# Two early row tiles turned by DMA instead of TensorE, and the order of the work around the first block's second query projection

## The chip, the cores and the metric

The kernel runs on one core of one Trainium2 chip. The metric is the device time of one execution in microseconds (us); less is better. Engines: PE is TensorE (PEld its weight loads), DVE is VectorE, ACT is ScalarE, POOL is GpSimd, SP is SyncE, which here only issues DMA. DMA transfers run on 16 DMA engines; those issued by SP show as queue q1, those issued by POOL as queue q0.

## The reference

The input x is 2048 rows of 640. It is normalized over its columns, and two branches read the result: attention with 32 heads of width 192 against given keys and values of 2048 rows, and a gated feed-forward layer of width 1536. Cut to what matters:

```python
xn = _layernorm(x, axis=-1)
q = (xn @ wq)                      # 32 heads of 192
scores = q @ k_cache^T * 192**-0.5
p = softmax(scores, axis=-1)
s = (p @ v_cache) @ wo             # A
g = silu((silu(xn @ w1) * (xn @ w3)) @ w2)   # B
return x + s * g
```

All inputs are bfloat16.

## The kernel before, in words

The rows of x come as 16 tiles of 128. Each tile is normalized in its natural layout and then turned, so that xnT holds its 640 columns on the partitions (five blocks of 128 columns), since the projections contract over them. The 2048 query rows are worked in four blocks (qb) of 512, that is four row tiles each. The heads run one after another; within a head and a block, the keys go in eight pairs of 128-row tiles. For each pair, `scores` issues six matmuls into a two-bank PSUM tile, `weights` takes the exponential on ScalarE, and `values` returns two closures ("parts") of eight matmuls each which add to two output banks. The two-bank tile comes from a pool of two buffers (`st2`) that the scores, the projections and the turns share in rotation; the third scores of the start borrow an output bank.

TensorE and most other instructions are pinned (`pin`): each engine runs them in the order in which the program emits them. This order was written by hand. The change lies in the first 50 us, in head 0, where the normalization of the later tiles runs beside the attention of the first block.

Normalizing a tile has these steps, each a small function:

- `load_x(eng, t0, t1)` loads tiles t0 to t1-1 (L188).
- `ln_stats(i)` issues two `ln_half`, each a statistics instruction over half the columns (L213), the second with an aggregate (L215), on VectorE.
- `ln_root(i0, n)` takes the reciprocal root of n tiles' variances on ScalarE, as a logarithm (L243) and an exponential (L250).
- `ln_scale(i0, n)` subtracts the mean and scales, on VectorE, into an `xn` buffer (L261; a pool of four).
- Then the tile is turned, in one of two ways. `next_turn(i0, cp)` makes ten transposes on TensorE for two tiles into PSUM (L270), and copies each tile to xnT with the engine given (L271). `ln_send(i0, n)` scales and issues one DMA transpose per tile from SP's queue, from `xn` straight to xnT (L282).

`first_project(h, qb, *mid)` projects the queries of head h for block qb through `project_chunk`. For head 0 and qb > 0 it uses `by_halves` (L328): ten matmuls, then a small copy as a fence (`mark`, L334; on ScalarE for block 1, on VectorE for the others) that waits for them, then whatever `between` emits, and then ten matmuls that wait for the fence. The results are cast on ScalarE into qA and qF (L361, L362), POOL makes the shifted copies qS and qD, VectorE takes maxima, and `next_bound` makes the block's shift for the exponential. For other heads the 20 matmuls run at L359 and read also xnS, a copy of xnT with its halves swapped, which `swap_rows` makes by DMA from POOL's queue (L380).

`lead()` is the hand-written start of block 0: pairs 0 to 4, with the statistics of tiles 4 to 11 and the turning of tiles 4 to 7 between. Behind it, `advance` takes the further pairs; it keeps up to three parts waiting (four with an extra step) and emits the rest. `extra_at` hangs an extra step on a pair, `posts` hangs steps behind it. Before, the projection of block 1 hung on pair (0, 5), with the root of tiles 8 to 10 and the sending of 8 and 9 in its middle.

Ahead of `lead()` stand, on SP's queue, the loads of x for tiles 8 to 11 and 12 to 15, and on POOL's queue the weights of head 1 and the swap of block 0 (`loads[1] = load_weights(1)`, `swap_rows(0)`).

Of the kernel before, what the change touches and what calls it, by code (L numbers as in the profile page):

```python
# [30 lines left out]
def _kernel_impl(ctx, tc, A_x, A_k_cache, A_v_cache, A_wq, A_wo, B_w1, B_w3, B_w2, out):  # L31
    nc = tc.nc
    _, SQ, D = A_x.shape
    _, H, SK, dh = A_k_cache.shape
# [7 lines left out]
    NPAIR = NKT // 2  # L42
# [111 lines left out]
    with ExitStack() as actx:  # L154
# [32 lines left out]
        def load_x(eng, t0, t1):  # L187
            pin(eng.dma_start(out=x_all[:, t0:t1, :], in_=x2[t0 * P:t1 * P, :].rearrange("(t p) d -> p t d", p=P)))  # L188
# [7 lines left out]
        loads[0] = load_keys(0, [first_w["pieces"][0], lambda: [f() for f in first_w["pieces"][1:]], lambda: [load_x(nc.sync, t, t + 2) for t in (4, 6)]])  # L196
        loads[0].update(first_w)
        load_x(nc.sync, 8, 12)
        load_x(nc.sync, 12, 16)

        fill = ps_o.tile([P, 2, 512], F32, tag="ob1", name="fill")

# [14 lines left out]
        def ln_stats(i):  # L217
            for a in range(nsub):
                ln_half(i, a)
# [36 lines left out]
        def ln_scale(i0, n=2):  # L256
            scaled[i0] = []
            for i in range(i0, i0 + n):
                xn = xnp.tile([P, D], BF16, tag="xn", name="xn")
                act = i in ASUM  # L260
                pin(nc.vector.tensor_scalar(out=xn[:], in0=x_all[:, i, :], scalar1=a_col(nmean, i) if act else mv[:, i, 0:1],  # L261
                                            scalar2=rstd[i], op0=ALU.add if act else ALU.subtract, op1=ALU.mult))
                scaled[i0].append(xn)
# [11 lines left out]
        def next_turn(i0, cp):  # L275
            for copy in ln_turn(i0, (cp, cp)):
                copy()
# [41 lines left out]
        def by_halves(banks, w, qs, touch, between):  # L319
            def behind_of(op, dep):  # L320
                tc.add_manual_dep(op.ins, dep.ins.name, mybir.DependencyInfo(
                    mybir.DependencyClass.Sync, mybir.DependencyReason.DATA), reason="bank")

            for half in range(2):
                for c in range(DC):
                    for r in range(2):
                        t = r ^ half
                        mm = pin(nc.tensor.matmul(banks[t], lhsT=w(t, c)[ROWS[r], :], rhs=xnT[ROWS[r], c, qs],  # L328
                                                  start=(half == 0 and c == 0), stop=(half == 1 and c == DC - 1)))
                        if half == 1 and c == 0:  # L330
                            behind_of(mm, fence)
                if half == 0:
                    mark = fsb.tile([P, 1], F32, tag="mark", name="mark")
                    fence = pin(touch(out=mark[:], in_=eps_t[:]))  # L334
                    behind_of(fence, mm)
                    between()

        def project_chunk(h, qb, cast=nc.vector.tensor_copy, mid=()):
            hd = heads[h]
            wq = hd["L"]["wq"]  # L340
            qA, qF, qS, qD, st = hd["qA"], hd["qF"], hd["qS"], hd["qD"], hd["st"]
            qs = slice(qb * 512, (qb + 1) * 512)
            ps = ps_st.tile([P, 1024], F32, tag="st2", name="ps")
            halves = [ps[:, 0:512], ps[:, 512:1024]]
            if h == 0 and qb > 0:
                by_halves(halves, lambda t, c: wq[:, t, c, :], qs, nc.scalar.copy if qb == 1 else nc.vector.tensor_copy, steps((parts.pop(0),), *mid))
            elif h == 0:
                acc["bp"] = ps_o.tile([P, 2, 512], F32, tag="ob0", name="bp")
                halves[1] = acc["bp"][:, 1, :]
                for u in (slice(0, 256), slice(256, 512)):  # L350
                    for t in range(2):
                        for c in range(DC):
                            pin(nc.tensor.matmul(halves[t][:, u], lhsT=wq[:, t, c, :], rhs=xnT[:, c, u],
                                                 start=(c == 0), stop=(c == DC - 1)))
            else:
                for s in range(2 * DC):
                    for t in range(2):
                        xs = xnT if s % 2 == t else xnS
                        pin(nc.tensor.matmul(halves[t], lhsT=wq[ROWS[t], s, :], rhs=xs[ROWS[t], s // 2, qs],  # L359
                                             start=(s == 0), stop=(s == 2 * DC - 1)))  # L360
            pin(cast(out=qA[:, qs], in_=halves[0]))  # L361
            pin(cast(out=qF[:, qs], in_=halves[1]))  # L362
            keep = pin if h == 0 or h == 1 else (lambda x: x)
            for t in range(2):
                keep(nc.gpsimd.tensor_copy(out=qS[ROWS[t], qs], in_=qA[ROWS[1 - t], qs]))  # L365

            first = h == 0 and qb == 0
            copy = nc.scalar.copy if first else nc.gpsimd.tensor_copy
            keep(copy(out=qD[:, qs], in_=qF[PGW:P, qs]))

            def maxima():
                for col, src, r0 in ((3, halves[0] if first else qA[:, qs], 0), (4, halves[1] if first else qF[:, qs], PGW)):
                    pin(nc.vector.tensor_reduce(out=st[r0:P, col, qb:qb + 1], in_=src[r0:P, :], axis=AX.X, op=ALU.max,
                                                apply_absolute_value=True))
            return maxima
# [110 lines left out]
        def weights(st2, nb):  # L486
            pT2 = pp.tile([P, 1024], BF16, tag="pT2", name="pT2")
            pin(nc.scalar.activation(out=pT2[:], in_=st2[:], func=ACT.Exp, scale=SCALE, bias=nb[:]))  # L488
            return pT2
# [107 lines left out]
        def steps(*fs):  # L597
            return lambda: [f(*a) for f, *a in fs]

        def lead():  # L600
            hd, nb = heads[0], heads[0]["nb"][0]
            vals = [values(hd, 0, p, weights(st2, nb), p < 2) for p, st2 in enumerate(early)]
            for i in (4, 5, 6, 7):
                ln_stats(i)
            ln_half(8, 0)
            vals[0].pop(0)()
            vals.append(values(hd, 0, 3, weights(scores(hd, 0, 3), nb)))
            vals[1].pop(0)()
            ln_root(4, 4)
            st2 = scores(hd, 0, 4)  # L610
            vals.append(values(hd, 0, 4, weights(st2, nb)))
            for v in vals[:4]:
                while v:
                    v.pop(0)()
            for i in (4, 6):
                ln_scale(i)
            ln_half(8, 1)
            next_turn(4, nc.scalar.copy)
            next_turn(6, nc.vector.tensor_copy)
            for v in vals[4]:  # L620
                v()
            for i in (9, 10):
                ln_stats(i)
            ln_half(11, 0)

        posts = {
            (0, 5): ((ln_send, 10, 1), (ln_half, 11, 1)),
            (1, 0): ((ln_root, 11, 1), (ln_send, 11, 1)),
            (1, 2): ((ln_stats, 12), (ln_stats, 13), (swap_rows, 1)),
            (1, 3): ((ln_stats, 14), (ln_stats, 15), (swap_rows, 2)),  # L630
            (2, 1): ((swap_rows, 3),),
        }
        extra_at = {
            (0, 5): ((first_project, 0, 1, (ln_root, 8, 3), (ln_send, 8)),),
            (1, 1): ((first_project, 1, 0),),
            (1, 4): ((first_project, 0, 2, (ln_root, 12, 4), (ln_send, 12), (ln_send, 14)),),
            (2, 1): ((first_project, 1, 1),),
            (2, 4): ((first_project, 0, 3),),
            (3, 1): ((first_project, 1, 2),),
            (3, 4): ((first_project, 1, 3),),  # L640
        }
# [3 lines left out]
        for qb in range(NQB):  # L645
            if qb == 0:
                lead()
            for p in range(5 if qb == 0 else 0, NPAIR):
                ex = extra_at.get((qb, p))
                advance(heads[0], qb, p, steps(*ex) if ex else None)  # L650
                if (qb, p) in behind_at:
                    behind.pop(0)()
                for f, *a in posts.get((qb, p), ()):
                    f(*a)
                if (qb, p) == (1, 5):
                    heads[1]["L"].update(load_keys(1, hold=True))
                if (qb, p) in ((1, 5), (1, 6), (1, 7)):
                    heads[1]["L"]["rest"].pop(0)()
                if (qb, p) == (2, 6):
                    loads[2] = load_keys(2, hold=True)  # L660
                    pin(nc.vector.memset(loads[2]["KT"][:, :, 0:2], 0.0))
                    loads[2]["rest"].pop(0)()
                if (qb, p) == (2, 7):
                    copy_keys(heads[1]["L"])
                    loads[2].update(load_weights(2))
                if (qb, p) in key_at:
                    next_keys(1, key_slots)
                if (qb, p) == (3, 6):
                    finish_head(1)
# [445 lines left out]
```

## Time and profile before

| | us |
|---|---|
| median of 3 runs | 1938.49 (1938.24 to 1938.61) |
| profiled execution, its own time | 1938.35 |
| its span, first to last instruction | 1936.6 |
| TensorE busy | 1927.2 |
| ScalarE busy | 1214.5 |
| VectorE busy | 1094.5 |
| GpSimd busy | 459.9 |

A profile line of the timeline has start, duration, engine, line, operation, what it writes and reads, and the count of instructions merged in it; in brackets stands how long the engine had been idle before it and what ended that. Lines with a q behind the engine's name (SPq, POOLq) are DMA issues. The granted TensorE clock is 0.999 of full over the run.

### The profile page before, as it was taken

To read this page: it belongs to the slowest core of one execution; us is meant where nothing else is said; L and a number is where in the kernel's file an instruction comes from. 1 tells how busy PE (TensorE), PEld (TensorE's weight loads), DVE (VectorE), ACT (ScalarE), POOL (GpSimd) and SP (SyncE) were. 2 spreads that over 40 slices of the span, in tenths; PEclk is the share of its full clock that TensorE was granted. 3 is DMA by queue.
4 is the path that set the end of the run, shared out by engine and by line. 5 is a ranking of instruction groups with operands and counts; after the bars stand their busy time and mean duration, and the time that the engine had idled before them with its cause. 6 is when DMAs were issued, how large, how long until landed. Compare 5 with 4: busy or idle time off the path is not lost.

```text
span 1936.6 us, 59523 instructions
## 1 busy us (share of the span) xinstructions
PE 1927.2 (100%) x26720; PEld 1264.5 (65%) x26743; DVE 1094.5 (57%) x2240; ACT 1214.5 (63%) x1173; POOL 459.9 (24%) x757
## 2 busy tenths in 40 slices
PE   9999999999999999999999999999999999999998
PEld 5666666666666666666666677666666666454455
DVE  8665666565656565656665666656665655521111
ACT  7777777777767677777777777777777777210000
POOL 3432222222222222233222222222222210000000
PEclk9999999999999999999999999999999999999999
DMA  8721223121212222232222222212131102937763
GB/s 171 134 71 41 80 42 79 42 71 39 63 37 68 49 57 60 58 95 68 63 50 71 50 71 49 71 41 79 42 79 41 39 10 94 270 81 146 164 152 76
DMA packets 340375, 148.34 MB, mean 77 GB/s; under 512 B 291649, under 2 KB 333601, under 8 KB 340113
## 3 DMA queue, kind: packets, MB, share of 16 engines
q1 hardware_dynamic: 327152, 114.84, 25.8%
q0 software_dynamic: 8256, 24.58, 4.7%
q10 hardware_dynamic: 4704, 5.05, 0.8%
q8 instruction: 211, 3.46, 0.8%
q14 instruction: 52, 0.42, 0.1%
HBM read 54.26 MB, written 31.98 MB: 45 GB/s over the span
## 4 chain that ended last, share of the span: by engine, by line
PE 99%; SPq 0%; DMA 0%; POOL 0%; ACT 0%; issue 0%; DVE 0%
PE obank L528 35%; PE st L482 34%; PE ps L359 14%; PE ps_s L885 8%; PE ps_s L841 3%; PE ps_f L905 2%; PE ps_gu L698 1%; PE ps_f L921 1%; PE ps L723 0%; PE ps L328 0%; DMA KT<-in_A_k_cache_dram 0%; SPq L114 0%; PE ps_gu L328 0%; SPq L98 0%; PE pst L270 0%
## 5 line engine op out<-in xcount | busy, mean ns | idle before, releaser
L488 ACT ACTIVATE pT<-st,nb 128x1024 bf16<-128x1024 f32 x1016 | 1131.8, 1114 | 434.2 <-PE st L482 433.7
L528 PEld LDWEIGHTS <-pT 64*128 64x128 bf16 x16384 | 713.1, 94 | 242.6 <-ACT pT L488 1.5
L528 PE MATMUL obank<-vt,pT 64*128 64x193 bf16 x16384 | 851.8, 243 | 0.1
L498 DVE COPY osum<-obank 128x386 f32<-128x386 f32 x256 | 142.4, 556 | 548.7 <-PE obank L528 548.5
L482 PE MATMUL st<-qS,KM 64*128 64x512 bf16 x1023 | 384.6, 376 | 0.7 <-ACT qF L362 0.5
L482 PE MATMUL st<-qS,KT 64*128 64x512 bf16 x1023 | 384.6, 376 | 0.1
L482 PE MATMUL st<-qA,KM 64*128 64x512 bf16 x1023 | 384.7, 376 | 0.0
L482 PE MATMUL st<-qD,KT 64*128 64x512 bf16 x1023 | 384.7, 376 | 0.0
L482 PE MATMUL st<-qF,KT 64*128 64x512 bf16 x1023 | 384.6, 376 | 0.0
L482 PE MATMUL st<-qA,KT 64*128 64x512 bf16 x1023 | 384.6, 376 | 0.0
L365 POOL COPY qS<-qA 64x512 bf16<-64x512 bf16 x256 | 189.4, 740 | 513.7 <-DVE qA L361 481.9
L482 PEld LDWEIGHTS <-KT 64*128 64x128 bf16 x4096 | 201.4, 94 | 136.2 <-issue 0.6
L359 PE MATMUL ps<-xnT,wq 64*128 64x512 bf16 x1240 | 288.0, 376 | 0.0
L359 PE MATMUL ps<-xnS,wq 64*128 64x512 bf16 x1240 | 287.0, 376 | 0.0
L359 PEld LDWEIGHTS <-wq 64*128 64x128 bf16 x2480 | 120.1, 94 | 116.6
L505 DVE TENSOR_TENSOR ostage<-osum,rl_all 128x384 bf16<-128x384 f32 x256 | 152.6, 596 | 8.8
L885 PE MATMUL ps_s<-oT,wo_sb 128*128 128x512 bf16 x705 | 154.9, 379 | 0.8
L499 DVE TENSOR_TENSOR osum<-osum,obank 128x386 f32<-128x386 f32 x256 | 142.6, 557 | 8.9
L885 PEld LDWEIGHTS <-wo_sb 128*128 128x128 bf16 x720 | 70.5, 98 | 84.9 <-issue 0.2
L384 DVE TENSOR_REDUCE st<-KT 128x1 f32<-128x512 bf16 (+1 forms) x189 | 122.0, 685 | 1.2
L482 PEld LDWEIGHTS <-KM 64*128 64x128 bf16 x2048 | 100.6, 94 | 17.2 <-issue 1.1
L103 POOL DMA_DIRECT2D wq<-in_A_wq_dram x62 | 45.8, 739 | 272.6 <-PE ps L359 260.3
(136 smaller groups left out, 1179.9 us busy)
## 6 DMA issues: line engine op xcount, KB each, us to landing
o_scr<-ostage SPq DMA_DIRECT2D x64, 384.0 KB, 2.9
vt<-in_A_v_cache_dram SPq DMA_DIRECT2D x62, 384.0 KB, 4.9
wo_sb<-in_A_wo_dram POOLq DMA_DIRECT2D x1, 7680.0 KB, 31.7
wq<-in_A_wq_dram POOLq DMA_DIRECT2D x31, 160.0 KB, 3.3
hT_scr<-hblk SPq DMA_DIRECT2D x16, 256.0 KB, 3.0
xnS<-xnT POOLq DMA_DIRECT2D x8, 320.0 KB, 7.0
wq<-in_B_w_dram POOLq DMA_DIRECT2D x31, 80.0 KB, 2.6
wq<-in_A_wq_dram POOLq DMA_DIRECT2D x31, 80.0 KB, 2.9
```

The lines of the kernel that those rows point to most:

```text
L103: keep(nc.gpsimd.dma_start(out=wq[ROWS[t], :, c0:c1], in_=w.rearrange("(s p) d -> p s d", p=DT)))
L359: pin(nc.tensor.matmul(halves[t], lhsT=wq[ROWS[t], s, :], rhs=xs[ROWS[t], s // 2, qs], start=(s == 0), stop=(s == 2 * DC - 1)))
L365: keep(nc.gpsimd.tensor_copy(out=qS[ROWS[t], qs], in_=qA[ROWS[1 - t], qs]))
L384: pin(nc.vector.tensor_reduce(out=heads[h]["st"][:, j, k:k + 1], in_=heads[h]["L"]["KT"][:, j, c0:c1], axis=AX.X, op=ALU.max, apply_absolu ...
L482: pin(nc.tensor.matmul(st2[:, t * 512:(t + 1) * 512], lhsT=k, rhs=q[ROWS[t], qs], start=(s == 0), stop=(s == 2)))
L488: pin(nc.scalar.activation(out=pT2[:], in_=st2[:], func=ACT.Exp, scale=SCALE, bias=nb[:]))
L498: pin(nc.vector.tensor_copy(out=osum[:], in_=ov[:, 0, :, 0:DH + 1]))
L499: pin(nc.vector.tensor_tensor(out=osum[:], in0=osum[:], in1=ov[:, 1, :, 0:DH + 1], op=ALU.add))
L505: pin(nc.vector.tensor_tensor(out=ostage[:, b * 2:b * 2 + 2, hg * DH:(hg + 1) * DH], in0=osum[:, :, 0:DH], in1=rl.unsqueeze(2).to_broadcas ...
L528: pin(nc.tensor.matmul(acc["o"][b][:, r, (j % 2) * 256:(j % 2) * 256 + DH + 1], lhsT=pT2[ROWS[r], t * 512 + j * P:t * 512 + (j + 1) * P], ...
L841: pin(nc.tensor.matmul(ps, lhsT=oT[:, k, :], rhs=wo_sb[:, k, c0:c1], start=(k == 0), stop=(k == OC - 1)))
L885: pin(nc.tensor.matmul(ps_of[d], lhsT=wo_sb[:, k, d * P:(d + 1) * P], rhs=part(k // KQ)[:, k % KQ, :], start=(k == 0), stop=(k == OC - 1)))
```

## The change

Tiles 4 and 5 get a root of their own, between the exponentials of pairs 1 and 2, and go by `ln_send` (DMA transpose) instead of `next_turn`. Tiles 6 and 7 get a root behind the scores of pair 4 and are still turned on TensorE, in one PSUM tile, copied by VectorE. The load of tiles 12 to 15 is issued behind the two DMA transposes instead of behind the load of 8 to 11. Pair 5's scores and exponential go ahead of the projection of block 1, pair 6's between its halves; the root of 8 to 10 and the sending of 8 and 9 go behind the projection, and the parts of pairs 4 to 6 behind that. `posts` of (0, 5) hang on (0, 7). In `project_chunk`, `by_halves` no longer pops a part by itself; for blocks 2 and 3 the caller passes it (`next_part`).

```diff
@@ start of the program @@
         load_x(nc.sync, 8, 12)
-        load_x(nc.sync, 12, 16)
@@ project_chunk @@
-                by_halves(halves, ..., steps((parts.pop(0),), *mid))
+                by_halves(halves, ..., steps(*mid))
@@ lead @@
+        def next_part():
+            parts.pop(0)()
+
         def lead():
             hd, nb = heads[0], heads[0]["nb"][0]
-            vals = [values(hd, 0, p, weights(st2, nb), p < 2) for p, st2 in enumerate(early)]
-            for i in (4, 5, 6, 7):
-                ln_stats(i)
+
+            def pair(p, st2=None):
+                if st2 is None:
+                    st2 = scores(hd, 0, p)
+                return values(hd, 0, p, weights(st2, nb), p < 2)
+
+            vals = [pair(p, st2) for p, st2 in enumerate(early[:2])]
+            ln_stats(4)
+            ln_stats(5)
+            ln_root(4, 2)
+            vals.append(pair(2, early[2]))
+            ln_half(6, 0)
+            ln_send(4)
+            ln_half(6, 1)
+            ln_stats(7)
+            load_x(nc.sync, 12, 16)
+            vals[0].pop(0)()
+            vals.append(pair(3))
+            vals[1].pop(0)()
+            st2 = scores(hd, 0, 4)
             ln_half(8, 0)
-            vals[0].pop(0)()
-            vals.append(values(hd, 0, 3, weights(scores(hd, 0, 3), nb)))
-            vals[1].pop(0)()
-            ln_root(4, 4)
-            st2 = scores(hd, 0, 4)
-            vals.append(values(hd, 0, 4, weights(st2, nb)))
+            ln_root(6, 2)
+            vals.append(pair(4, st2))
             for v in vals[:4]:
                 while v:
                     v.pop(0)()
-            for i in (4, 6):
-                ln_scale(i)
+            ln_scale(6)
             ln_half(8, 1)
-            next_turn(4, nc.scalar.copy)
             next_turn(6, nc.vector.tensor_copy)
-            for v in vals[4]:
-                v()
+            vals.append(pair(5))
             for i in (9, 10):
                 ln_stats(i)
             ln_half(11, 0)
+            first_project(0, 1, (lambda: vals.append(pair(6)),))
+            ln_root(8, 3)
+            ln_send(8)
+            for v in vals[4:]:
+                parts.extend(v)
+            for _ in range(4):
+                next_part()
 
         posts = {
-            (0, 5): ((ln_send, 10, 1), (ln_half, 11, 1)),
+            (0, 7): ((ln_send, 10, 1), (ln_half, 11, 1)),
...
         extra_at = {
-            (0, 5): ((first_project, 0, 1, (ln_root, 8, 3), (ln_send, 8)),),
...
-            (1, 4): ((first_project, 0, 2, (ln_root, 12, 4), (ln_send, 12), (ln_send, 14)),),
+            (1, 4): ((first_project, 0, 2, (next_part,), (ln_root, 12, 4), (ln_send, 12), (ln_send, 14)),),
...
-            (2, 4): ((first_project, 0, 3),),
+            (2, 4): ((first_project, 0, 3, (next_part,)),),
...
-            for p in range(5 if qb == 0 else 0, NPAIR):
+            for p in range(7 if qb == 0 else 0, NPAIR):
```

More of the change, by code (lines that the diff above doesn't have):

```diff
@@ L345, in project_chunk @@
             if h == 0 and qb > 0:
-                by_halves(halves, lambda t, c: wq[:, t, c, :], qs, nc.scalar.copy if qb == 1 else nc.vector.tensor_copy, steps((parts.pop(0),), *mid))
+                by_halves(halves, lambda t, c: wq[:, t, c, :], qs, nc.scalar.copy if qb == 1 else nc.vector.tensor_copy, steps(*mid))
             elif h == 0:
```

## The prediction

> **What bounds the kernel now.** I read the page first, then the list of who waited for whom on TensorE, then the timelines of TensorE, ScalarE, VectorE and the SP queue from 11 to 48 us, and last the packets of each DMA queue in stretches of that time.
>
> ```profile
> PE 1927.2 (100%) x26720; PEld 1264.5 (65%) x26743; DVE 1094.5 (57%) x2240; ACT 1214.5 (63%) x1173; POOL 459.9 (24%) x757
> PE 99%; SPq 0%; DMA 0%; POOL 0%; ACT 0%; issue 0%; DVE 0%
> ```
>
> ```profile
> PE fill L205 <- DVE cols L170: 1.6, 1, 1.6
> PE st L482 <- ACT qF L362: 0.5, 1, 0.5
> ```
>
> TensorE is busy for 1927.2 of 1936.6 us and is 99% of the chain that ended last. Its list of waits has, behind the start, one entry of 0.5 us at 26 us and two smaller ones. So nothing later gives lost time back: what the first 40 us lose or gain on TensorE stands in the total one for one. A change here is worth the TensorE work that it removes, less the waits that it makes.
>
> **What the change removes from TensorE.**
>
> ```profile
> 17.43 2.18 PE L528 MATMUL obank<-vt,pT 64*128 64x193 bf16 x48
> 19.54 1.33 PE L270 MATMUL pst<-ident_bf,xn 128*128 128x128 bf16 x20
> 22.29 1.26 PE L328 MATMUL ps<-xnT,wq 64*128 64x512 bf16 x10
> 24.02 1.24 PE L328 MATMUL ps<-xnT,wq 64*128 64x512 bf16 x10
> 37.69 0.61 PE L328 MATMUL ps<-xnT,wq 64*128 64x512 bf16 x4
> ```
>
> The 20 transposes of tiles 4 to 7 occupy 19.54 to 20.80, 1.26 us; ten of them go, 0.63 us. With the 0.5 us wait for qF gone too, and some 0.3 us around the fence, the gain could not pass 1.5 us. That is the bound on the good side, and it is less than 0.2% of the time (3.88 us, about what a measurement of this kernel can tell from no change).
>
> Order matters more than work. Before, two parts of pair 4 and the scores of pair 5 stood between the turns and the projection of chunk 1 (22.29). After, the parts go behind the projection, pair 5's scores alone stay ahead, and pair 6 stands between its halves. TensorE runs its list in order, so whatever the first half waits for stops everything. It needs tiles 6 and 7 from VectorE's copies and tiles 4 and 5 from the DMA.
>
> **The near inputs: ScalarE and VectorE.**
>
> ```profile
> 14.26 2.12 ACT L488 ACTIVATE pT<-st,nbb 128x1024 bf16<-128x1024 f32 x2 [1.39 <-DVE nbb L427]
> ...
> 18.27 0.30 ACT L243 ACTIVATE lv<-mv,eps_t 128x4 f32<-128x4 f32 x1
> ...
> 18.71 1.10 ACT L488 ACTIVATE pT<-st,nbb 128x1024 bf16<-128x1024 f32 x1
> ...
> 25.30 0.59 ACT L361 CAST qA<-ps 128x512 bf16<-128x512 f32 x1 [0.91 <-PE ps L328]
> ```
>
> ```profile
> 15.17 0.83 DVE L213 BATCH_NORM_STATS2 st<-x_all 128x6 f32<-128x320 bf16 x2
> 16.04 0.21 DVE L215 BATCH_NORM_AGGREGATE mv<-st 128x2 f32<-128x12 f32 x1
> ...
> 18.84 1.51 DVE L261 TENSOR_SCALAR xn<-x_all,mv,rstd 128x640 bf16<-128x640 bf16 x4 [0.25 <-ACT rstd L250]
> 20.27 0.48 DVE L213 BATCH_NORM_STATS2 st<-x_all 128x6 f32<-128x320 bf16 x1
> ...
> 20.92 0.87 DVE L271 COPY xnT<-pst 128x640 bf16<-128x640 bf16 x2
> ...
> 24.43 0.80 DVE L261 TENSOR_SCALAR xn<-x_all,mv,rstd 128x640 bf16<-128x640 bf16 x2 [0.25 <-ACT rstd L250]
> ...
> 28.96 0.21 DVE L215 BATCH_NORM_AGGREGATE mv<-st 128x2 f32<-128x12 f32 x1
> 29.31 0.56 DVE L498 COPY osum<-obank 128x386 f32<-128x386 f32 x1
> ...
> 37.47 0.15 DVE L334 COPY mark<-eps_t 128x1 f32<-128x1 f32 x1
> ```
>
> A root costs ScalarE 0.44 us (18.27 to 18.71). The early root of 4 and 5 can start at about 16.3, when tile 5's statistics end (16.04 + 0.21) and the two exponentials end (14.26 + 2.12). It pushes the exponential of pair 2 back by 0.44, so the third bank frees later and the 48 matmuls of 17.43 start at about 17.85. VectorE fills the gap with half of tile 6 and scales tile 4 from about 16.88 to 17.27 (1.51 / 4 each), tile 5 to 17.65. The rest of 6, tile 7 and half of 8 follow, about 1 us per tile; the root of 6 and 7 then starts near 19.4, their scaling ends near 20.75, the other half of tile 8 near 21.35, and the two copies (0.87) near 22.25. On TensorE the ten transposes end at about 21.05 and pair 5's scores at 21.7. So without any DMA wait the projection starts at about 22.3, where it starts now: the saved 0.63 us lies in a wait for VectorE.
>
> ScalarE loses two copies there, no longer on anyone's path. A VectorE copy of a turned tile is 0.43 against its 0.65, which is priced already.
>
> **The far input: two transposes by DMA.** Tile 4's can be issued at about 17.35 (the scaled tile plus the 0.07 us that 24.43 + 0.40 to 24.90 shows). What they cost depends on what is in the DMA engines then.
>
> ```profile
> 11.51 1.56 SPq L188 DMA_DIRECT2D x_all<-in_A_x_dram  x2
> 24.90 1.57 SPq L282 DMA_TRANSPOSE xnT<-xn  x1
> 38.56 2.87 SPq L282 DMA_TRANSPOSE xnT<-xn  x1
> 41.53 1.91 SPq L282 DMA_TRANSPOSE xnT<-xn  x1
> ```
>
> ```profile
> xnT<-xn SPq DMA_TRANSPOSE x1, 2.7
> xnT<-xn SPq DMA_TRANSPOSE x1, 7.8
> xnT<-xn SPq DMA_TRANSPOSE x1, 5.4
> ```
>
> The three landing times belong to the issues at 24.90, 38.56 and 41.53. The first met idle engines. The other two followed the swaps that POOL issued, and landed at 46.36 and 46.93. The queues show why; the stretches are 12 to 18, 18 to 24.5 and 36 to 42 us (packets, MB, share of the 16 engines):
>
> ```profile
> q1 hardware_dynamic: 2395, 2.05, 105.2%
> q0 software_dynamic: 14, 0.06, 2.3%
> ```
>
> ```profile
> q0 software_dynamic: 338, 0.93, 70.2%
> ```
>
> ```profile
> q0 software_dynamic: 355, 1.24, 87.7%
> q1 hardware_dynamic: 53, 0.01, 1.6%
> ```
>
> ```profile
> 13.20 1.04 POOL L103 DMA_DIRECT2D wq<-in_A_wq_dram  x1
> 15.67 1.38 POOL L380 DMA_DIRECT2D xnS<-xnT  x2
> ...
> 35.21 2.88 POOL L380 DMA_DIRECT2D xnS<-xnT  x4
> ```
>
> POOL issues head 1's weights from 13.20 and two swaps from 15.67 to 17.05, but its queue moves 0.06 MB before 18: the loads that SP issued earlier go first. From 36 to 42 it is the other way round: a transpose issued at 38.56 moves 0.01 MB until the swaps are through. Here the engines serve in order of issue.
>
> Moving the load of 12 to 15 (0.66 MB of the 2.05 that took 6 us) lets POOL's 0.93 MB start about 1.9 us sooner: about 16 to 21, its stragglers to 22.3. Tile 4's transpose at 17.35 comes 0.3 us behind the last of it, as that of 38.56 came 0.5 us behind the last of the swaps issued to 38.09, and as much lies ahead of it. So I take the contended pair, the nearest rows: tile 5 lands 41.53 + 5.4 - 38.56 = 8.37 us after tile 4's issue, at 25.72, and the projection starts at 25.75. The other bound is two transposes alone, 1.67 us apart (the second of the pair at 24.90 was issued at 26.57): 17.35 + 1.67 + 2.7 = 21.7, no wait. TensorE then stands from 21.7 to 25.75, with nothing to cover it. First term: 25.75 - 22.29 = **3.46 us**.
>
> SP has the load of 12 to 15 queued behind the transposes. Even issued at 23 it lands long before its statistics, which now start at 33.39 and start later after: nothing.
>
> **Behind the projection.** The casts came 3.01 us after its first matmul (25.30 - 22.29); after, pair 6's scores take the place of the part, its exponential ends as the second half ends: 3.0 again. From there VectorE is the chain: maxima, bound, tile 10 and 11, two evictions, statistics of 12 to 15 and the fence of chunk 2 at 37.47, with one gap of 0.14 (28.96 + 0.21 to 29.31); chunk 2's second half starts right behind that fence (37.69). The change puts the scaling of 8 and 9 (0.80) from ahead of the maxima to behind them, inside this run. Less the gap: **0.6 us**. Tile 11's transpose lands about 13 us after the projection starts and chunk 2 wants it after about 14: nothing, by a small margin. POOL's copies and its bound stand as far behind the casts as before. The parts taken at chunks 2 and 3 are only called otherwise: nothing.
>
> Sum: 3.46 + 0.6 = 4.06 us. The profiled execution took 1938.35 us (span 1936.6 and 1.75 around it), 0.14 below the median of the runs; 1938.35 + 4.06 = **1942.4 us**.
>
> **Rivals.** *The queues share.* If the engines alternate between the queues, each transpose loses about 1 us to POOL's packets: tile 5 lands near 21.7 + 1.5 = 23.2, and the loss is 0.9 + 0.6 = 1.5: 1939.9 us, not slower. It decides at a landing before 25.5. The rows of 12 to 18 and 36 to 42 speak against it; for it, stragglers of both queues run together after 18. By the Trainium skill (DMA: Bandwidth & Descriptors, Queues, rings and completion order) each engine does go round the queues packet by packet; by that rule the time would be near this rival's, and the two stretches do not agree with it.
>
> *The clock falls.*
>
> ```profile
> 1.65 1.86 PE L205 MATMUL fill<-ones_w,ones_bf 128*128 128x512 bf16 x4 [1.65 <-DVE cols L170]
> 6.67 0.81 PE L205 MATMUL fill<-ones_w,ones_bf 128*128 128x512 bf16 x3
> ```
>
> After the idle start the fills run about 0.43 us apart, later about 0.22. If TensorE comes out of a 4 us wait at that half rate for as long as at the start (some 3.4 us: 4.72 us for 13 fills), the projection loses 1.7 us more: 4.06 + 1.7 = 5.8, 1944.1 us. Against it: no wait of this length stands in the trace. The Trainium skill (TensorE: Matmul & The Clock Gate, Part 1) has the clock halve after an idle window of about 3.4 us that runs free; the cold fills agree with its rate, and no row here shows a fall inside the kernel.
>
> *The DMA is early.* Both land by 22.3, and only VectorE's 0.6 or a part of the 1.5 us gain is left: -0.5 to +0.6, 1938.4 us. It needs POOL's queue empty at about 20.
>
> *Tile 11 late.* Should the swaps of chunk 1 overtake its transpose, chunk 2 waits 1 to 2 us more: about 1944.
>
> **How the numbers follow.** Forecast 0.42, of which 0.28 above the bound and 0.14 below, since 4.06 stands so near 3.88; clock 0.17; sharing 0.24; early 0.10; tile 11 late 0.05; and 0.02 for a gain of over 0.2% that no row explains. Slower 0.28 + 0.17 + 0.05 = 0.50; same 0.14 + 0.24 + 0.10 = 0.48; faster 0.02. The range goes from 1938.7 (early, with VectorE's part) to 1945.3 (clock, 1.2 us more for a later landing). The likeliest case alone: 1941.3 to 1943.4.
>
> **What would show it.** Right: a TensorE wait of about 4 us ahead of the first L328 near 22, ended by the DMA of xnT; POOL's queue from 16, tile 4's packets only after 20; the first half at 25 to 26, chunk 2's second half at 41 to 42. Sharing: both transposes landed by 24. Clock: L328 matmuls at double spacing behind the wait. Wrong altogether: a projection that starts by 22.3.

## The result, and the profile after

The changed kernel takes 1942.97 us (median of 14 runs, 1940.58 to 1944.84), the kernel before 1938.54 us (14 runs, 1938.12 to 1939.48). The ratio is 1.0022, 95% interval 1.0014 to 1.0029: slower by 4.43 us. The profiled execution took 1943.48 us, its span is 1941.7 us (1936.6 before). Not only the median moved: the runs spread over 4.3 us where those of before spread over 1.4.

The page's busy times and its chain, and TensorE's list of waits (who waited for whom: total us, times, longest):

```profile
PE 1928.7 (99%) x26710; PEld 1266.3 (65%) x26733; DVE 1093.9 (56%) x2240; ACT 1212.9 (62%) x1173; POOL 458.5 (24%) x757
PE 98%; DVE 1%; DMA 0%; ACT 0%; issue 0%; POOL 0%
```

```profile
PE ps L327 <- DMA xnT<-xn: 2.8, 1, 2.8
PE fill L204 <- DVE cols L170: 1.6, 1, 1.6
PE ps L327 <- DVE mark L333: 0.5, 1, 0.5
```

Ten matmuls fewer were issued, yet TensorE was busy 1.5 us longer. Two waits are new: 2.8 us for the DMA ahead of block 1's projection, and 0.5 us for VectorE's fence at block 2's. TensorE's timeline:

```profile
25.13 1.82 PE L327 MATMUL ps<-xnT,wq 64*128 64x512 bf16 x10 [2.82 <-DMA xnT<-xn]
...
27.99 1.81 PE L327 MATMUL ps<-xnT,wq 64*128 64x512 bf16 x10
29.62 1.51 PE L527 MATMUL obank<-vt,pT 64*128 64x193 bf16 x32
...
42.95 1.25 PE L327 MATMUL ps<-xnT,wq 64*128 64x512 bf16 x10 [0.52 <-DVE mark L333]
```

The ten matmuls that took 1.24 to 1.26 us before take 1.8 now. The stretches of 1 us show why; behind the busy times and counts of PE, PEld, DVE, ACT and POOL stand the granted TensorE clock, the DMA engines' share and GB/s:

```profile
25.00:26.00 1.00, 0.87 (x8) 0.51 (x10) 0.00 (x0) 0.00 (x0) 0.00 (x0) 0.84 1.07 361
26.00:27.00 1.00, 1.00 (x8) 0.42 (x6) 0.00 (x0) 0.01 (x1) 0.00 (x0) 0.50 0.25 81
28.00:29.00 1.00, 1.00 (x8) 0.52 (x6) 0.00 (x0) 0.73 (x1) 0.00 (x0) 0.50 0.00 0
29.00:30.00 1.00, 1.00 (x18) 0.63 (x15) 0.00 (x0) 0.54 (x2) 0.00 (x0) 0.95 0.07 16
```

The clock is half from about 25.68 (0.84 of that stretch) to 29.1 (0.95), that is for 3.4 us. It fell half a microsecond after the wait had ended. The projection, with pair 6's scores between its halves, took 4.49 us (25.13 to 29.62, where the next matmuls start).

The wait itself, on SP's queue, with the times from issue to landing of the two transposes behind it, and the queues in the stretches 18 to 19, 20 to 21 and 21 to 22 us:

```profile
17.68 2.75 SPq L281 DMA_TRANSPOSE xnT<-xn  x1
20.52 1.22 SPq L281 DMA_TRANSPOSE xnT<-xn  x1
```

```profile
xnT<-xn SPq DMA_TRANSPOSE x1, 6.7
xnT<-xn SPq DMA_TRANSPOSE x1, 4.5
```

```profile
q0 software_dynamic: 62, 0.13, 96.4%
q1 hardware_dynamic: 8, 0.01, 6.7%
...
q0 software_dynamic: 61, 0.20, 99.5%
q1 hardware_dynamic: 8, 0.00, 1.5%
...
q1 hardware_dynamic: 192, 0.05, 81.7%
q0 software_dynamic: 49, 0.15, 63.1%
```

Tile 4's transpose is issued at 17.68 and moves next to nothing until about 21, while POOL's weights and swap keep the engines busy for 96 to 100%; what is left of them (49 packets in the stretch to 22) then moves beside it. Tile 5's transpose lands at 25.0.

The sum can be closed on the timelines. Before, block 2's second half started at 37.69, now at 42.95: 5.26 us. The first scores came 0.35 later (12.98 against 12.63), ahead of anything that the change touches. The projection starts 12.15 us after them instead of 9.66: 2.49. The half clock gives 1.7 (below), VectorE's longer run the remaining 0.7. From there on nothing is lost or won: from the second half of block 3's projection to the end are 1883.92 us before (1936.6 - 52.68) and 1883.76 after (1941.7 - 57.94).

### The profile page after: what moved, and what is told of

Same layout as the page of the kernel before. It is cut to its first block, busy times and chain, and to the rows that moved or that the text cites. A ratio compares the mean times of both kernels' runs of the same rounds, so it can differ in the third digit from the quotient of the medians.

```text
span 1941.7 us, 59510 instructions
## 1 busy us (share of the span) xinstructions
PE 1928.7 (99%) x26710; PEld 1266.3 (65%) x26733; DVE 1093.9 (56%) x2240; ACT 1212.9 (62%) x1173; POOL 458.5 (24%) x757
## 3 DMA queue, kind: packets, MB, share of 16 engines
q8 instruction: 211, 3.46, 0.8%
## 4 chain that ended last, share of the span: by engine, by line
PE 98%; DVE 1%; DMA 0%; ACT 0%; issue 0%; POOL 0%
PE obank L527 35%; PE st L481 34%; PE ps L358 14%; PE ps_s L903 8%; PE ps_s L859 3%; PE ps_f L923 2%; PE ps_gu L716 1%; PE ps_f L939 1%; PE ps L741 0%; DVE st L212 0%; PE ps L327 0%; DMA xnT<-xn 0%; DVE xn L260 0%; DMA x_all<-in_A_x_dram 0%; PE ps_gu L327 0%
```

## Experiments

The theory: the two transposes come behind what POOL put into the DMA engines, TensorE idles, its clock falls, and VectorE's scaling of tiles 8 and 9 lengthens its run to block 2's fence. The rivals: DMA transposes are slow beside any traffic, the queues share by packets, or the new order itself costs the time. The differences below are between medians, each against the kernel before on the same chip. Where the interval of the ratio holds 1, the median alone doesn't tell the run from the kernel before, and the reading rests on the timelines, one profiled execution for each run.

**The swap behind tile 5.**

```diff
         loads[1] = load_weights(1)
-        swap_rows(0)
...
             load_x(nc.sync, 12, 16)   # in lead(); ahead of it:
+            behind5 = stt.tile([P, 1], BF16, tag="behind5", name="behind5")
+            pin(nc.gpsimd.tensor_copy(out=behind5[:], in_=xnT[:, DC - 1, 6 * P - 1:6 * P]))
+            swap_rows(0)
```

> The change, with POOL's swap of block 0 issued only once tile 5 has landed (a one-column copy on POOL reads it first). Theory (the two transposes wait for what POOL put into the DMA engines before them): without the swap only 0.33 MB of weights lies ahead, tile 5 lands near 22, the wait of 2.8 us ahead of the projection shrinks to under 0.5 us, TensorE's clock stays up, and the total is 1938.8 to 1939.5 with a narrow spread. Rival (a DMA transpose is slow by itself beside any traffic, or the queues share by packets): the wait stays above 2 us and the total above 1941.

Measured: 1939.49 us against 1938.76 (+0.73; ratio 1.0004, 0.9995 to 1.0013), 1938.65 to 1940.51. The transposes, and TensorE's waits:

```profile
17.84 1.25 SPq L281 DMA_TRANSPOSE xnT<-xn  x1
19.18 2.11 SPq L281 DMA_TRANSPOSE xnT<-xn  x1
```

```profile
xnT<-xn SPq DMA_TRANSPOSE x1, 4.2
xnT<-xn SPq DMA_TRANSPOSE x1, 3.5
```

```profile
PE ps L327 <- DVE mark L333: 0.5, 1, 0.5
PE pst L269 <- DVE xn L260: 0.3, 1, 0.3
PE ps L327 <- DVE xnT L270: 0.3, 1, 0.3
```

Tile 5 lands at 22.68, the 2.8 us wait is gone, and the projection starts 9.62 us after the first scores, as before (9.66). Of the 4.43 us, 3.7 hang on POOL's swap, which the change did not touch. What is left is VectorE's longer run, with the wait for the fence at its end.

**All four tiles on TensorE, in the new order.**

```diff
-            ln_send(4)
+            ln_scale(4)
...
+            next_turn(4, nc.scalar.copy)
             next_turn(6, nc.vector.tensor_copy)
```

> The change's order, but tiles 4 and 5 are turned on TensorE in a bank of their own ahead of 6 and 7, copied by ScalarE, instead of by DMA. Theory (the DMA is the cost, the order is not): no wait for a DMA, the projection of block 1 starts near 22.6 to 23 us, the total is 1938.9 to 1939.8. Rival (the new order itself, with the parts behind the projection, costs most): 1941 or more.

Measured: 1940.34 us (+1.58; 1.0008, 0.9999 to 1.0017), 1939.82 to 1940.62. Higher than expected, but far from the rival's 1941. The projection starts 10.12 us after the first scores; block 2's fence is late by 0.2, and pair 5's scores wait for a bank that ScalarE must first copy:

```profile
PE st L481 <- ACT xnT L270: 0.5, 1, 0.5
```

So the new order costs 1.58 us when TensorE also turns tiles 4 and 5, more than the 0.73 with two DMA transposes that have only head 1's weights ahead of them. Turning by DMA was not in itself the loss; what lay ahead of it in the DMA engines was.

**Matmuls in the wait.**

```diff
+            if h == 0 and qb == 1:      # in project_chunk, ahead of by_halves
+                for _ in range(12):
+                    pin(nc.tensor.matmul(halves[0], lhsT=ones_bf[:], rhs=ones_w[:], start=True, stop=True))
```

> The change, with twelve matmuls that compute nothing needed put on TensorE between pair 5's scores and the projection (2.6 us at full clock), so that TensorE isn't idle in the wait. Theory (the wait makes the clock fall to half for some 3.4 us, worth 1.7 us in most runs): the wait shows only a rest under 1 us, the clock stays at 1.0 from 25 to 30 us, the total falls to about 1941.2 and the spread of 4 us between runs shrinks to under 2. Rival (the slow matmuls behind the wait have another cause, such as the DMA traffic): the matmul spacing stays and the total stays near 1943.

Measured: 1941.96 us (+3.20; 1.0016, 1.0007 to 1.0026), with all runs between 1941.52 and 1942.94. TensorE's timeline, and the stretches 24 to 26 and 26 to 28 us:

```profile
25.59 1.25 PE L327 MATMUL ps<-xnT,wq 64*128 64x512 bf16 x10 [0.38 <-DMA xnT<-xn]
27.33 1.24 PE L327 MATMUL ps<-xnT,wq 64*128 64x512 bf16 x10
28.41 1.50 PE L530 MATMUL obank<-vt,pT 64*128 64x193 bf16 x32
```

```profile
24.00:26.00 2.00, 1.62 (x10) 0.58 (x10) 0.75 (x3) 0.00 (x0) 0.00 (x0) 1.00 1.15 286
26.00:28.00 2.00, 2.00 (x22) 0.90 (x20) 0.00 (x0) 0.66 (x2) 0.00 (x0) 1.00 0.42 139
```

The DMA is as late as ever (25.59), the clock stays at 1.00, and the projection takes 2.82 us (25.59 to 28.41) where it took 4.49: the half clock cost 1.67 us, and the slow matmuls were not the DMA traffic's doing. The excess over the kernel before falls by 1.2 us (4.43 to 3.20), not 1.7. In this profile the transposes landed later, 7.5 and 6.7 us after issue, and the projection began 12.80 us after the first scores instead of 12.15; that would make up the rest, but it compares one execution of each. With the clock kept up the spread falls from 4.3 to 1.4 us, so most of the difference between the runs came with the clock. One stretch at half rate costs 1.67 us, though, and what made up the rest of the 4.3 is not shown, since only one execution of the change has a trace.

**The load of 12 to 15 ahead of the transposes again.**

```diff
         load_x(nc.sync, 8, 12)
+        load_x(nc.sync, 12, 16)
...
-            load_x(nc.sync, 12, 16)
```

> The change, with the load of tiles 12 to 15 put back ahead of the two transposes. Theory (the engines serve in order of issue): POOL's traffic starts 1.3 to 2 us later, tile 5 lands at 26 to 27, the wait grows to 4 to 5 us, the total is 1944 to 1946. Rival (the queue's order doesn't matter here): no difference from the change, 1943.

Measured: 1945.24 us (+6.48; 1.0033, 1.0021 to 1.0045). The wait, and the stretches of 2 us:

```profile
PE ps L328 <- DMA xnT<-xn: 4.9, 1, 4.9
```

```profile
22.00:24.00 2.00, 0.00 (x0) 0.00 (x0) 1.93 (x7) 1.04 (x1) 0.40 (x1) 0.92 1.35 192
24.00:26.00 2.00, 0.00 (x0) 0.00 (x0) 0.44 (x2) 0.00 (x0) 0.00 (x0) 0.50 1.06 135
28.00:30.00 2.00, 2.00 (x12) 0.88 (x10) 0.00 (x0) 0.19 (x1) 0.00 (x0) 0.50 0.00 0
30.00:32.00 2.00, 2.00 (x27) 1.21 (x25) 0.00 (x0) 1.49 (x2) 0.00 (x0) 0.87 0.03 8
```

Moving the load was right by itself: without it the projection starts 2.05 us later (14.20 after the first scores against 12.15). The clock is half from about 23.7 to 30.5, twice 3.4 us, and falls within the wait here, 1.8 us after TensorE's last matmul (21.89).

**The sending of 8 and 9 back in the middle** (on top of the late swap).

```diff
-            first_project(0, 1, (lambda: vals.append(pair(6)),))
-            ln_root(8, 3)
-            ln_send(8)
+            first_project(0, 1, (lambda: vals.append(pair(6)),), (ln_root, 8, 3), (ln_send, 8))
```

> The late swap as in the first run, and the root and the sending of tiles 8 and 9 put back into the middle of block 1's projection, so that their scaling runs ahead of the maxima again. Theory (VectorE's unbroken run up to the fence of chunk 2 is 0.8 us longer by that scaling): the 0.5 us wait for that fence goes, the total falls by 0.4 to 0.7 us against the late swap alone, to 1938.8 to 1939.1. Rival (the fence waits for something else): the wait and the total stay.

Measured: 1939.15 us against 1938.61 (+0.54; 1.0001, 0.9992 to 1.0010). The wait for the fence is gone. From head 1's first projection to block 2's second half are 7.69 us, 8.29 with the late swap alone, 7.60 before: VectorE's run is confirmed at 0.6 to 0.7. But the root now stands ahead of the casts on ScalarE:

```profile
25.85 0.28 ACT L242 ACTIVATE lv<-mv,eps_t 128x3 f32<-128x3 f32 x1
26.17 0.20 ACT L249 ACTIVATE rstd<-lv 128x3 f32<-128x3 f32 x1
26.28 0.57 ACT L360 CAST qA<-ps 128x512 bf16<-128x512 f32 x1
```

The casts come 3.4 us after the projection's start (22.90) instead of 3.0, and 0.3 us of wait for qD is the price. The total missed the expected range by 0.05 us, and the gain on the late swap (0.73 to 0.54) is less than the 0.4 to 0.7 expected. Besides the casts, the DMA took a part of it here: with the same transfers ahead the transposes landed 4.4 and 3.7 us after issue, TensorE waited 0.6 us for them, and the projection began 9.90 us after the first scores instead of 9.62.

**The copies split between VectorE and ScalarE.**

```diff
-            ln_half(8, 1)
-            next_turn(6, nc.vector.tensor_copy)
-            vals.append(pair(5))
+            for copy in ln_turn(6, (nc.vector.tensor_copy, nc.scalar.copy)):
+                copy()
+            vals.append(pair(5))
+            ln_half(8, 1)
```

> As the run with the late swap and the sending in the middle, and the two turned tiles are copied one by VectorE and one by ScalarE ahead of the second half of tile 8's statistics, so that tiles 6 and 7 are in place about 0.6 us sooner. If tile 5's landing sets the start of the projection there too (9.5 us after the first scores), little is won: 0 to 0.2 us, and the profile shows a wait for the DMA in place of VectorE's. If VectorE alone set it: 0.5 us less, about 1938.4.

Measured: 1939.56 us (+0.95; 1.0005, 0.9996 to 1.0014). A miss, and for neither reason: tile 5 landed at 22.2 and the two copies ran one after the other, so that the projection began at 23.10, when ScalarE's was done.

```profile
22.36 0.69 ACT L270 COPY xnT<-pst 128x640 bf16<-128x640 bf16 x1 [0.90 <-DVE xnT L270]
```

**Head 1's weights behind tile 5 too.**

```diff
-        loads[1] = load_weights(1)
...
             pin(nc.gpsimd.tensor_copy(out=behind5[:], ...))
+            loads[1] = load_weights(1)
             swap_rows(0)
```

> As the run before, with head 1's weights issued behind tile 5 as well, so that nothing of POOL lies in the DMA engines when the two transposes come. Theory (issue order): tile 4 lands about 2.7 us and tile 5 about 4.2 us after tile 4's issue, the projection starts 9.1 us after the first scores at the latest, the total is 1938.2 to 1938.6, faster than the kernel before by 0 to 0.5 us. Rival (the late weights and swap now hold up the first projection of head 1): a wait of 0.5 us or more ahead of that projection near 30 us, 1938.8 or more.

Measured: 1939.53 us (+0.92; 1.0006, 0.9997 to 1.0015).

```profile
17.51 1.39 SPq L281 DMA_TRANSPOSE xnT<-xn  x1
19.00 1.22 SPq L281 DMA_TRANSPOSE xnT<-xn  x1
```

```profile
xnT<-xn SPq DMA_TRANSPOSE x1, 2.5
xnT<-xn SPq DMA_TRANSPOSE x1, 2.4
```

With nothing of POOL ahead, the transposes land in 2.5 and 2.4 us, tile 5 at 21.4, and TensorE no longer waits for them. That is the theory's clearest comparison: 6.7 and 4.5 behind weights and swap, 4.2 and 3.5 behind the weights alone (4.4 and 3.7, then 3.1 and 2.4, in the two runs after that), 2.5 and 2.4 behind nothing. From tile 4's issue to tile 5's landing that is 7.3 us, 4.3 to 5.1 us and 3.9 us. The total was missed because ScalarE's late copy set the start, 9.88 us after the first scores; head 1's projection did not wait for its late weights, though its swap landed only at 30.87, just ahead of the first matmul that reads it (30.93).

**Three more orders.** Both copies on VectorE, and the root and sending ahead of pair 6:

```diff
+            first_project(0, 1, (ln_root, 8, 3), (ln_send, 8), (lambda: vals.append(pair(6)),))
```

> Head 1's weights and the swap behind tile 5 as in the last run; both turned tiles copied by VectorE again, but ahead of the second half of tile 8's statistics; the root and the sending of 8 and 9 ahead of pair 6 in the middle of the projection, where ScalarE has a gap. Theory (with the DMA gone from the path, what is left are two near waits: ScalarE's copy that came behind VectorE's, 0.6 us, and qD behind the late casts, 0.3 us): the projection starts 9.4 to 9.6 us after the first scores, the qD wait goes, the total is 1938.5 to 1938.9, about the kernel before. Rival (the new order costs 0.5 us or more of its own in any form): 1939.2 or more.

Measured: 1939.35 us against 1938.68 (+0.67; 1.0004, 0.9995 to 1.0013). The start is as expected (9.59), the wait for qD is not gone: the root waited for tile 10's statistics and pushed pair 6's exponential and the casts back, to 4.0 us after the start.

```profile
25.07 0.30 ACT L242 ACTIVATE lv<-mv,eps_t 128x3 f32<-128x3 f32 x1 [1.12 <-DVE mv L214]
```

Then pair 4's parts ahead of the projection (`for v in vals[4]: v()` behind `pair(5)`, two `next_part` instead of four):

> As the run before, with the two parts of pair 4 put back ahead of the projection of block 1, where TensorE waits for VectorE's copies. If the chain behind the projection (casts, maxima, bound, first exponential of block 1) sets the time there, the start moves 0.3 us back and the total is 0 to 0.3 us more than without it; if TensorE's own work sets it, 0.3 us less: 1938.3 to 1938.6.

Measured: 1939.47 us (+0.79; 1.0004, 0.9995 to 1.0013): no difference that these runs can tell. The projection starts 9.83 us after the first scores instead of 9.59, as the first of the two cases has it. And a root for 8 and 9 alone:

```diff
+            ln_stats(9)
+            first_project(0, 1, (ln_root, 8, 2), (ln_stats, 10), (ln_send, 8), (lambda: vals.append(pair(6)),), (ln_half, 11, 0))
+            ln_root(10, 1)
```

> As the run with both copies by VectorE, but the root in the middle of the projection covers tiles 8 and 9 alone, so that it needn't wait for tile 10's statistics and the casts aren't pushed back; tile 10 gets its own root behind the casts. If the three terms are all there is (wait for DMA, VectorE's longer run, casts pushed back), none is left: the casts come 3.0 us after the first matmul of block 1's projection as in the kernel before, no wait for qD, and the total is 1938.3 to 1938.8, the same as the kernel before. If the order has a further cost: 1939.1 or more.

Measured: 1939.05 us against 1938.85 (+0.20; 1.0000, 0.9991 to 1.0010), the same as the kernel before; the median is 0.25 us over the expected range, though. ScalarE's rows, then the first matmuls of head 1's projection and the landing of the second swap, issued at 25.28:

```profile
24.45 0.30 ACT L242 ACTIVATE lv<-mv,eps_t 128x2 f32<-128x2 f32 x1
...
25.89 0.57 ACT L360 CAST qA<-ps 128x512 bf16<-128x512 f32 x1
```

```profile
30.54 0.37 PE L358 MATMUL ps<-xnT,wq 64*128 64x512 bf16 x1
31.04 0.39 PE L358 MATMUL ps<-xnS,wq 64*128 64x512 bf16 x2
```

```profile
xnS<-xnT POOLq DMA_DIRECT2D x1, 320.0 KB, 5.7
```

The casts come 3.05 us after the start (22.84), and with that the three terms are gone. A fourth is left: block 3's second half starts 40.33 us after the first scores, 40.05 before. The first matmul that reads the swap starts 0.50 us behind the one ahead of it, 0.10 in the run with both copies on VectorE, and the swap lands at 30.98, just ahead of it. So the late swap seems to hold up head 1's projection by some 0.4 us here, the rival of the run with the late weights; the list of waits doesn't name it. The 0.63 us of transposes saved never reached the total. Where the DMA was early enough, the projection began 9.56 to 9.88 us after the first scores, 9.66 before: there it waited for VectorE's or ScalarE's copy of tiles 6 and 7, or came behind pair 4's parts on TensorE. No version that was tried beats the kernel before.

## Why the prediction was right, and where it was not

The forecast was 1942.4 us and slower, the measurement 1942.97. The direction and the cause were right. That the sum fits so well is partly luck: the wait for the DMA came out 0.97 us shorter than its term, the clock took 1.67 us that the sum had put at nothing, and the median is that of runs which differ by 4.3 us.

*The near inputs.* Right: with the DMA out of the way (late swap) the projection starts 9.62 us after the first scores, 9.66 before.

*The far input.* Right in kind: the transposes waited for POOL's weights and swap, POOL's queue began at 16 to 17, tile 4's packets came after 21. The term was too large: tile 5 landed 7.3 us after tile 4's issue (17.68 to 25.0), where the contended pair before had 8.37; with the matmuls in the wait it was 8.0 (17.48 to 25.5). The issue itself came when it should, 4.70 us after the first scores (4.72 in the prediction). The loss was 2.49 instead of 3.46.

*The clock.* Given as a rival with a chance of 0.17, on the condition of a 4 us wait, and put at nothing in the sum. The step that failed is this condition: a wait of 2.8 us did it. The price, 1.7 us from the fills of the start, was measured as 1.67. That rival's total, 1944.1, and the forecast's hold the median between them. The prediction found no fall of the clock in the trace of the kernel before; there is one behind the last matmul, which ends at 1931.31:

```profile
1931.00:1931.50 0.50, 0.31 (x6) 0.14 (x3) 0.15 (x1) 0.00 (x0) 0.00 (x0) 1.00 0.74 248
1933.50:1934.00 0.50, 0.00 (x0) 0.00 (x0) 0.00 (x0) 0.00 (x0) 0.00 (x0) 0.77 0.04 16
```

The clock falls there at about 1933.8, 2.5 us into an idle time, so a wait well under 4 us was enough already then.

Not every run need have lost it. Two of the 14 (1940.58 and 1941.10 us) list a mean clock of 1.000 over the span, which leaves no room for a stretch like this one (1.67 us is 0.0009 of the span). For the others the mean doesn't settle it, since a fall behind the last matmul, which costs nothing, lowers it too.

By the Trainium skill (TensorE: Matmul & The Clock Gate, Part 1) the gate closes after an idle window of about 3.4 us that runs free. The lengths at half rate agree (3.4 us, and 6.8 with the load first). The fall has no fixed place either, as a window that runs free would have it. It came 3.4 us after TensorE's last matmul in the change, 1.8 with the load first, and behind the last matmul of the program 2.5 to 4.9 us after it in ten of the twelve profiles; in the other two it did not come in the 5.1 us that were left. But the wait was shorter than a window. If the window ends at the fall, it held about 0.6 us of matmuls in the change (22.31 to 25.13 is idle) and 1.6 us with the load first (20.33 to 21.89 is busy), and counted as idle all the same.

*VectorE's run.* 0.6 predicted, 0.7 measured: from the start of block 1's projection to block 2's second half are 17.82 us, 15.40 before, and of the 2.42 more 1.67 are the clock's. In the late swap's run, where the clock stays up, it is 0.7 too (8.29 against 7.60 from head 1's first projection on).

*The rival of sharing queues.* The runs with the late swap and with all of POOL's transfers late speak against it in this stage: each lot of POOL's traffic taken from ahead of the transposes brought them forward, and with it ahead they moved 8 packets from 20 to 21 us while POOL's queue moved 61. The rule of the Trainium skill (DMA: Bandwidth & Descriptors, Queues, rings and completion order), that each engine goes round the queues packet by packet, does not describe these rows; by it the time would have been near that rival's 1939.9. The order is not strict either: with the load first, POOL's queue moved 62 packets and SP's 81 from 18 to 19 us. Why POOL's earlier transfers go first was not separated from a plain order of issue.

*Tile 11* was not late: no wait ahead of block 2's first half.

*The range.* Its lower end, the early DMA with VectorE's part, comes to 1938.35 + 0.6 = 1938.95 us by the prediction's own rows, not 1938.7; nothing hangs on it.

## What to carry to other kernels

Before a step is moved from an engine that is always busy to the DMA, look at what every queue has issued by then, not at the landing time of the same transfer elsewhere: here 2.5 us became 6.7 behind another engine's transfers. A wait on TensorE costs its length and may cost a stretch at half clock behind it (1.67 us after a wait of 2.8), so matmuls that compute nothing can be worth their place in it. And work taken off the busiest engine brings nothing where its next start is set by a neighbour.

## What the runs showed of the hardware that was not expected

The clock fell after a wait of 2.82 us, 0.55 us after TensorE had gone on, and stayed at 0.50 for 3.4 us; a wait of 4.9 us brought 6.8 us at 0.50. Over all profiles the fall came 1.8 to 4.9 us after a last matmul, or not at all in 5.1 us. An issue of a DMA transpose held SP for 1.2 to 1.6 us with nothing of POOL ahead, and for 2.75 us behind POOL's traffic, where the next one took 1.22. The first scores come at 12.56 to 13.44 us in the profiles, though the code ahead of them is the same but for two POOL issues and a load: a difference between single executions, of the size of the effects sought here.
